# Both feed-forward products of a retention block computed with one level of Strassen's algorithm

## The chip, the core and the metric

The kernel runs on one core of a Trainium2 chip. The metric is device time in microseconds (us), from the launch of the program to its end on that core. The core has a matrix engine (PE, with the weight loads shown as PEld), a vector engine (DVE), a scalar engine (ACT), a general engine (POOL), and a queue (SP) that issues the transfers between DRAM and on-chip memory. PE reads its operands from on-chip memory and writes to eight banks of accumulators (PSUM), each 512 float32 wide on 128 partitions; DVE and ACT read these banks.

## What is computed

```python
# q, k, v: (4, 8, 768, 64); w_in: (512, 2048); w_out: (2048, 512)
for t in range(S):
    state = gamma * state + einsum('bhd,bhe->bhde', k[:, :, t], v[:, :, t])
    y[:, :, t] = scale * einsum('bhd,bhde->bhe', q[:, :, t], state)
x = y.transpose(0, 2, 1, 3).reshape(3072, 512)
h = x @ w_in
g = where(h > 0, h, exp(minimum(h, 0)) - 1)     # ELU
out = g @ w_out
```

Each head has its own decay gamma. All values are float32. The weights arrive as 64-bit floats and are turned into 32-bit floats on the chip, by integer operations on their two halves ("decoding").

## The kernel before

The 3072 tokens are cut into 24 chunks of 128 for the attention and into 6 blocks of 512 for the feed-forward part; a block is four chunks. For a chunk, `scores` (L189) multiplies keys and queries, DVE masks the result into `pt` (L192), and `values` multiplies `pt` with the values (L212), adds the contribution of the running state (L230), updates that state (L221 on PE, L243 to L246 on DVE) and writes one quarter of the block's input `xt` (L236). The scores have two PSUM banks of their own (`ps_s`), the values two others (`ps_y`), the state one (`ps_c`), the feed-forward products three (`ps_f`).

For a block, `ffn` computes 16 feed-forward tiles, each four matmuls of 128x128 weights with 512 tokens (L257), and turns each into `g` with one exponential on ACT (L262) and two operations on DVE (L263, L265). Then come 4 output tiles, each 16 matmuls with 512 columns of `w_out` (L273), a copy out of PSUM on ACT (L280) and a store. PE runs every float32 matmul as two passes, each with its own weight load, so a block has 128 passes of each product and the kernel 1536.

The order of the work is written out: Python generators issue the instructions, and each engine works through its own in that order. `ffn` yields after every feed-forward tile and every quarter of an output tile, 32 times a block; the loop at the end puts one chunk of the next block's attention into every eighth of these steps, and issues that chunk's loads on SP.

The weights come as 32 pieces of 128 x 512 words. `decode` needs one operation on ACT (L107), four on DVE (L110 to L114) and an integer addition on POOL (L115) for each. The first four pieces are decoded between the first four chunks, before any feed-forward tile; the others two at a time, after each of the first block's feed-forward tiles. `scale_v` multiplies a chunk's values by the inverse decay, on DVE for the first four chunks and on POOL (L176) after that.

Of the kernel before, what the change touches and what calls it, by code (L numbers as in the profile page):

```python
# [8 lines left out]
FP32 = mybir.dt.float32  # L9
# [7 lines left out]
def kernel(  # L17
# [3 lines left out]
    w_bits: bass.AP,  # L21
    out: bass.AP,
    dims,
):

# [14 lines left out]
    TB = 512  # L40
    HP = H // 2
# [4 lines left out]
    KJ = DM // P  # L46
    NFT = DFF // P
    assert D == 64 and DM == H * D == 512 and KJ == HP == 4 and S % C == 0 and NTOK % TB == 0
# [5 lines left out]
    ldpool = ctx.enter_context(tc.tile_pool(name="ldpool", bufs=4))  # L54
    wraw = ctx.enter_context(tc.tile_pool(name="wraw", bufs=4))
    wtmp = ctx.enter_context(tc.tile_pool(name="wtmp", bufs=2))
    ppool = ctx.enter_context(tc.tile_pool(name="ppool", bufs=2))
    spool = ctx.enter_context(tc.tile_pool(name="spool", bufs=2))
    xpool = ctx.enter_context(tc.tile_pool(name="xpool", bufs=2))
    gpool = ctx.enter_context(tc.tile_pool(name="gpool", bufs=NFT + 2))  # L60
    epool = ctx.enter_context(tc.tile_pool(name="epool", bufs=2))
    opool = ctx.enter_context(tc.tile_pool(name="opool", bufs=2))
    ps_s = ctx.enter_context(tc.tile_pool(name="ps_s", bufs=2, space=PSUM))
    ps_y = ctx.enter_context(tc.tile_pool(name="ps_y", bufs=2, space=PSUM))
    ps_c = ctx.enter_context(tc.tile_pool(name="ps_c", bufs=1, space=PSUM))
    ps_f = ctx.enter_context(tc.tile_pool(name="ps_f", bufs=3, space=PSUM))
# [5 lines left out]
    def load(m):  # L72

        if m >= NCHUNK:
            return
        qk = ldpool.tile([P, 2, HP, C], FP32, name="qk", tag="qk")
        nc.sync.dma_start(qk.rearrange("p a h c -> p (a h c)"), qkv[m, :, 0:1024])
        kv = ldpool.tile([C, 2, H, D], FP32, name="kvn", tag="kvn")
# [4 lines left out]

    w_in_sb = [const.tile([P, KJ, P], FP32, name=f"w_in{f}") for f in range(NFT)]
    w_out_sb = [const.tile([P, DM], FP32, name=f"w_out{f}") for f in range(NFT)]
    pieces = [w.rearrange("p a b -> p (a b)") for w in w_in_sb] + list(w_out_sb)
    NPIECE = len(pieces)
    staged, decoded = [], []

    def load_piece():  # L90
        n = len(staged)
        if n < NPIECE:

            t = wraw.tile([P, 512, 2], U32, name="wraw", tag="wraw")
            nc.sync.dma_start(t.rearrange("p c w -> p (c w)"), w_bits[n].bitcast(U32))
            staged.append(t)

    def decode(upto):
# [3 lines left out]
        vec = nc.vector  # L102
        while len(decoded) < min(upto, NPIECE):
            t, dst = staged[len(decoded)], pieces[len(decoded)].bitcast(U32)
            lo, hi = t[:, :, 0], t[:, :, 1]
            r = wtmp.tile([P, 512], U32, name="wr", tag="wr")
# [241 lines left out]
```

## Times and profile before

| | |
|---|---|
| time, median of 3 runs | 791.96 us (789.93 to 792.26) |
| time of the profiled execution | 793.54 us |
| its span, first to last instruction | 791.6 us |
| PE busy | 754.7 us, 95% |
| DVE, ACT, POOL busy | 251.5, 94.3 and 64.7 us |
| mean granted clock of PE | 0.987 |

Times in the rows are microseconds from the start of the span unless marked ns. A busy PE is not PE at its peak: the duration of a matmul in the trace (592 ns for 512 columns) holds its way through the array, during which the next one already runs. The pace of the passes is read from where successive ones start, or from a chain of waits, whose pieces don't overlap. PEld shows the weight loads beside the passes. An engine's idle time counts only where another engine waits for it.

### The profile page before, as it was taken

The page shows a single profiled execution, that of the slowest core. Times are in us where ns is not written, and L with a number is a line of the kernel's source. Part 1 is how long each engine was busy: PE and PEld are TensorE (multiplying, and loading weights), DVE is VectorE, ACT ScalarE, POOL GpSimd, SP SyncE. Part 2 cuts the span into 40 slices and gives each one's busy share as a digit, 9 for nine tenths or more (in the row PEclk, how much of TensorE's full clock was granted, in tenths as well). Part 3 has the DMA queues.
Part 4 walks back from the last instruction along what each step waited for, and adds up shares of the span by engine and source line. Part 5 has one row for each costly group of instructions (what it writes and reads, how often), then busy time and mean ns, then how long its engine had stood idle before and what let it go on. Part 6 is the DMA issues. An engine that isn't in the chain of part 4 may idle for free.

```text
span 791.6 us, 7134 instructions
## 1 busy us (share of the span) xinstructions
PE 754.7 (95%) x2944; PEld 358.9 (45%) x2944; DVE 251.5 (32%) x484; ACT 94.3 (12%) x158; POOL 64.7 (8%) x60
## 2 busy tenths in 40 slices
PE   6876669999999999999999999999999999999998
PEld 6432224444444444444544444444444444444443
DVE  6999994012342001333100433100333101133000
ACT  2222221001110000111000111000111000111000
POOL 1433443000000000000000000000000000000000
PEclk9999898999999999999999999999999999999999
DMA  9846450210101101101102001111000000000000
GB/s 344 325 157 211 159 187 0 80 64 17 54 8 46 67 26 67 53 1 54 66 14 80 28 26 53 45 37 67 14 1 0 3 24 14 13 1 0 14 13 26
DMA packets 15007, 48.68 MB, mean 61 GB/s; under 512 B 1664, under 2 KB 1664, under 8 KB 14976
## 3 DMA queue, kind: packets, MB, share of 16 engines
q1 hardware_dynamic: 14976, 48.24, 17.3%
q8 instruction: 23, 0.38, 0.2%
q14 instruction: 8, 0.07, 0.0%
HBM read 41.94 MB, written 6.29 MB: 61 GB/s over the span
## 4 chain that ended last, share of the span: by engine, by line
PE 86%; DVE 10%; issue 2%; DMA 2%; SPq 0%; ACT 0%; ACTq 0%
PE op L273 43%; PE hp L257 35%; DVE wc L112 3%; PE sc L189 3%; PE y L212 3%; DVE wc L110 2%; DVE wc L113 2%; DVE wc L114 1%; PE y L230 1%; PE kv L221 1%; DMA kvn<-in_qkv_dram 1%; DMA qk<-in_qkv_dram 1%; DVE pt L192 1%; DVE e L263 1%; DVE xt L236 0%
## 5 line engine op out<-in xcount | busy, mean ns | idle before, releaser
L257 PE MATMUL hp<-xt,w_in 128*128 128x512 f32 x768 | 342.3, 602 | 21.7 <-DVE g L265 21.1
L273 PE MATMUL op<-w_out,g 128*128 128x512 f32 x768 | 339.0, 599 | 3.0 <-DVE g L265 3.0
L257 PEld LDWEIGHTS hp<-xt,w_in 128*128 128x128 f32 x768 | 145.2, 192 | 204.0 <-issue 201.8
L273 PEld LDWEIGHTS op<-w_out,g 128*128 128x128 f32 x768 | 145.2, 191 | 182.1 <-issue 180.5
L263 DVE TENSOR_SCALAR e<-e 128x512 f32<-128x512 f32 x96 | 42.2, 439 | 242.6 <-ACT e L262 242.6
L262 ACT ACTIVATE e<-hp 128x512 f32<-128x512 f32 x96 | 57.1, 596 | 263.3 <-PE hp L257 263.3
L265 DVE TENSOR_TENSOR g<-hp,e 128x512 f32<-128x512 f32 x96 | 66.4, 692 | 4.0
L192 DVE TENSOR_TENSOR pt<-sc,cmask 128x512 f32<-128x512 f32 x48 | 30.8, 684 | 115.4 <-PE sc L189 115.4
L280 ACT COPY ot<-op 128x512 f32<-128x512 f32 x24 | 14.1, 586 | 351.3 <-PE op L273 351.3
L176 POOL TENSOR_TENSOR kvn<-kvn,vf 128x512 f32<-128x512 f32 x20 | 21.3, 1071 | 406.6 <-DMA kvn<-in_qkv_dram 378.8
L236 DVE TENSOR_TENSOR xt<-y,etab 128x256 f32<-128x256 f32 x48 | 18.4, 419 | 112.0 <-PE y L230 91.7
L189 PE MATMUL sc<-qk 64*128 64x128 f32 x384 | 30.6, 298 | 6.3 <-DMA qk<-in_qkv_dram 5.7
L189 PEld LDWEIGHTS sc<-qk 64*128 64x128 f32 x384 | 25.6, 198 | 22.3 <-issue 15.2
L107 ACT ACTIVATE wr<-wraw 128x512 uint32<-128x512 uint32 x32 | 21.8, 681 | 78.5 <-POOL w_out L115 33.6
L212 PE MATMUL y<-pt,kvn 128*64 128x128 f32 x384 | 27.8, 290 | 2.3 <-DVE xt L236 2.3
L212 PEld LDWEIGHTS y<-pt,kvn 128*64 128x64 f32 x384 | 21.7, 142 | 18.2 <-issue 13.9
L112 DVE TENSOR_SCALAR wc<-wc 128x512 f32<-128x512 f32 x32 | 27.6, 863 | 1.1
L115 POOL TENSOR_TENSOR w_in<-wc,wr 128x512 uint32<-128x512 uint32 x16 | 21.5, 1344 | 48.0 <-DVE wc L114 44.2
L115 POOL TENSOR_TENSOR w_out<-wc,wr 128x512 uint32<-128x512 uint32 x16 | 21.0, 1312 | 30.6 <-DVE wc L114 28.6
L114 DVE SCALAR_TENSOR_TENSOR wc<-wraw,wc 128x512 uint32<-128x512 uint32 x32 | 22.2, 693 | 1.1
L110 DVE TENSOR_SCALAR wc<-wraw 128x512 uint32<-128x512 uint32 x32 | 17.0, 531 | 0.1
L113 DVE TENSOR_SCALAR wc<-wc 128x512 uint32<-128x512 uint32 x32 | 13.7, 427 | 1.1
(26 smaller groups left out, 73.9 us busy)
## 6 DMA issues: line engine op xcount, KB each, us to landing
wraw<-in_w_dram SPq DMA_DIRECT2D x32, 512.0 KB, 3.3
qk<-in_qkv_dram SPq DMA_DIRECT2D x24, 512.0 KB, 4.1
kvn<-in_qkv_dram SPq DMA_DIRECT2D x24, 512.0 KB, 4.9
out_dram<-ot SPq DMA_DIRECT2D x24, 256.0 KB, 2.0
```

The lines of the kernel that those rows point to most:

```text
L110: vec.tensor_scalar(c, hi, 0x7FFFFFFF, None, ALU.bitwise_and)
L112: vec.tensor_scalar(cf, cf, 122879.9921875, 2.0**-15, ALU.min, ALU.max)
L114: vec.scalar_tensor_tensor(c, hi, 0xC0000000, c, ALU.bitwise_and, ALU.bitwise_or)
L115: nc.gpsimd.tensor_tensor(out=dst, in0=c, in1=r, op=ALU.add)
L189: nc.tensor.matmul(sc[a][:, p, :], lhsT=qk[r, 1, p, :], rhs=qk[r, 0, p, :], start=True, stop=True)
L192: nc.vector.tensor_tensor(out=pt[:, a], in0=sc[a], in1=cmask.unsqueeze(1).to_broadcast([C, HP, C]), op=ALU.mult)
L212: nc.tensor.matmul(y[a][c * D : (c + 1) * D, u, :], lhsT=vn[:, h, :], rhs=pt[:, a, p, :], start=(u == 0), stop=(i == 0), skip_group_check= ...
L257: nc.tensor.matmul(hp, lhsT=w_in_sb[ft][:, j, :], rhs=xt[:, j, :], start=(j == 0), stop=(j == KJ - 1))
L262: nc.scalar.activation(e, hp, AF.Exp)
L263: nc.vector.tensor_scalar(e, e, 1.0, -1.0, ALU.min, ALU.add)
L265: nc.vector.tensor_tensor(out=gt, in0=hp, in1=e, op=ALU.max)
L273: nc.tensor.matmul(op, lhsT=g[ft][:, c * P : (c + 1) * P], rhs=w_out_sb[ft], start=(ft == 0), stop=(ft == NFT - 1),)
```

## The change

The first block keeps the ordinary products. From the second block on, both products are cut in halves on all three sides, and seven products of the halves replace eight: the left and right sides are the quarters of the weights and of the input, or sums and differences of quarters, and the results are combined afterwards. The seven are called 1 to 7; `strassen` issues them in the order 1, 2, 6, 7, 5, 3, 4.

- For `h = x @ w_in` (`first`), the 16 tiles are taken four at a time, as n = 0 to 3. A product is four matmuls of 128x128 weights with 256 tokens, 8 passes. Three accumulators (pa, pb, pd) hold two tiles of 128 x 256 each. ACT copies three intermediate sums out of pa (m1, u2, u4), DVE adds them to the results of 2, 5 and 4 (`plus`, L347), and ELU takes two operations on ACT (L280, L281) and one on DVE (L283) for each of the results C11, C22, C12 and C21. Two more operations on DVE make the differences T3 and T1 (L403). Products 3 and 4 of one n are issued after products 1 and 2 of the next one.
- For `out = g @ w_out` (`second`), each product is 16 matmuls, 32 passes. Its weights, 1 MB, are fetched from a DRAM scratch (`fetch`, L418) into three buffers that the raw weights used before. The four chunks of attention for the next block stand behind products 2, 6, 7 and 5.
- The first block's second product (`plain_second`) takes the pieces of `w_out` as they are decoded, keeps four accumulators open, forms the combinations of `w_out` on DVE (L313, four operations of 128x256 for each of eight pieces) and writes both to the scratch; `combine_w_in` forms those of `w_in` in place (L329, four operations of 128x512 for each n). All four chunks of the second block's attention stand in this product.
- A piece of weights is now 128 x 1024 words, 16 in all. `decode` uses two operations on ACT and four on DVE, the last being the integer addition (L130), and none on POOL. Two pieces are decoded between the first four chunks, eight during the first product, six during the second. ELU's new form also holds in the first block.
- The decay is no longer applied chunk by chunk to the state: the tables `vf` and `etab` hold it for all 768 positions, the state accumulates in PSUM, and ACT copies it out. Scores and values share two PSUM banks after the first block (tag "s"), and the feed-forward products have five.

```diff
+    def decode():
+        n = len(decoded)
...
+        nc.scalar.activation(cf, hi.bitcast(FP32), AF.Abs)
+        vec.tensor_scalar(cf, cf, 122879.9921875, 2.0**-15, ALU.min, ALU.max)
+        vec.tensor_scalar(c, c, 3, 0x3FFFFFF8, ALU.logical_shift_left, ALU.bitwise_and)
+        vec.scalar_tensor_tensor(c, hi, 0xC0000000, c, ALU.bitwise_and, ALU.bitwise_or)
+        nc.scalar.activation(flat, lo, AF.Copy, scale=2.0**-29)
+        vec.tensor_tensor(out=flat, in0=c, in1=flat, op=ALU.add)
...
+        ps, tag = (ps, "f") if ps else (ps_s, "s")
+        y = [ps.tile([P, 2, C], FP32, name="y", tag=tag) for _ in range(2)]
...
+    def elu(g, h):
+        r = epool.tile([P, 512], FP32, name="r", tag="r")
+        nc.scalar.activation(r, h, AF.Relu, scale=-1.0)
+        nc.scalar.activation(r, r, AF.Exp, scale=-1.0)
+        flush()
+        later.append(lambda: nc.vector.scalar_tensor_tensor(g, r, -1.0, h, ALU.add, ALU.max))
...
+    def strassen(product, use, between):
+        yield
+        pa = bank()
+        product(1, pa, True)
+        m1 = kept(pa)
+        yield
+        pb = bank()
+        product(2, pb, True)
+        use("C11", plus(pb, m1))
+        yield
+        product(6, pa, False)
+        u2 = kept(pa)
+        yield
+        pd = bank()
+        product(7, pd, True)
+        yield
+        product(5, pa, False)
+        u4 = kept(pa)
+        use("C22", plus(pd, u4))
+        yield "gap"
+        product(3, pa, False)
+        use("C12", pa)
+        yield
+        product(4, pd, False)
+        use("C21", plus(pd, u2))
...
+            elu(flat(g), flat(h))
+            gq[name] = g
+            if name == "C12":
+                flush()
+                t3_ = gpool.tile([P, 2, TH], FP32, name="g", tag="g")
+                sub(t3_, gq["C22"], gq["C12"])
+                sub(gq["C12"], gq["C12"], gq["C11"])
...
+    for tb in range(1, NTB):
+        gqs = [{} for _ in range(NQ)]
+        for n in range(NQ):
+            cur = first(n, gqs[n])
+            for at in range(3):
+                next(cur)
+            for _ in tail:
+                pass
+            for s in cur:
+                if s == "gap":
+                    break
+            tail = cur
+        cur = second(tb, gqs)
+        next(cur)
+        next(cur)
+        for _ in tail:
+            pass
+        flush()
+        m = (tb + 1) * CPB
+        scale_v(m)
+        scores(m)
+        for j in range(4):
+            s = next(cur)
+            scale_v(m + j + 1) if j < 3 else None
+            values(m + j)
+            load(m + j + 2)
+            if j < 3:
+                scores(m + j + 1)
```

In the orders below one row is a float32 matmul, not one of its two passes. On PE, before, a feed-forward tile is one row of four matmuls with 512 columns:

```order
L257 MATMUL hp<-xt,w_in_99 128x512 x4
L257 MATMUL hp<-xt,w_in_100 128x512 x4
L189 MATMUL sc<-qk 128x128 x8
L257 MATMUL hp<-xt,w_in_101 128x512 x4
```

Now, for n = 1 of a block's first product; ps_997 is pa and ps_1021 is pd of n = 0, ps_1039, ps_1046 and ps_1087 are pa, pb and pd of n = 1:

```order
L390 MATMUL ps_1039<-xb_168,w_a1_94 128x256 x4
L390 MATMUL ps_1046<-xb_168,w_a1_94 128x256 x4
L390 MATMUL ps_997<-xb_168,w_s0_101 128x256 x4
L390 MATMUL ps_1021<-xt3_172,w_b0_97 128x256 x4
L390 MATMUL ps_1039<-xt1_170,w_s1_102 128x256 x4
L390 MATMUL ps_1087<-xt2_171,w_s1_102 128x256 x4
L390 MATMUL ps_1039<-xt0_169,w_b1_98 128x256 x4
```

The matmuls now have half as many columns, and stand as products 1, 2 of n = 1, 3, 4 of n = 0, and 6, 7, 5 of n = 1.

On ACT, in the same place: the copies m1 (m_1044), u2 (m_1085) and u4 (m_1096) of n = 1, and between them the ELU steps of C11 of n = 1 (r_1054), C12 (r_1063, from PSUM) and C21 (r_1078) of n = 0:

```order
L342 COPY m_1044<-ps_1039 128x512
L280 ACTIVATE r_1054<-h_1051 128x512
L281 ACTIVATE r_1054<-r_1054 128x512
L280 ACTIVATE r_1063<-ps_997 128x512
L281 ACTIVATE r_1063<-r_1063 128x512
L280 ACTIVATE r_1078<-h_1075 128x512
L281 ACTIVATE r_1078<-r_1078 128x512
L342 COPY m_1085<-ps_1039 128x512
L342 COPY m_1096<-ps_1039 128x512
```

Before, ACT had one operation for a feed-forward tile; here the copy u2, for which product 5 waits, stands behind six ELU steps.

On PE, in a block's second product, around the second chunk of attention (one row of L427 is a product):

```order
L427 MATMUL ps<-g,ws 128x256 x16
L227 MATMUL y<-pt,kvn 64x128 x8
L237 MATMUL kv<-kvn 64x64 x8
L247 MATMUL y<-qk,state 64x128 x8
L204 MATMUL sc<-qk 128x128 x8
L427 MATMUL ps<-g,ws 128x256 x16
```

Before, matmuls of the feed-forward part stood between one chunk's values and the next chunk's scores; now the scores (L204) follow the values directly, in the same two banks.

## Rows read from the trace of the kernel before

**Rows 1.** Page, part 1: busy time, share of the span, instructions; part 4: chain.

```profile
PE 754.7 (95%) x2944; PEld 358.9 (45%) x2944; DVE 251.5 (32%) x484; ACT 94.3 (12%) x158; POOL 64.7 (8%) x60
...
PE 86%; DVE 10%; issue 2%; DMA 2%; SPq 0%; ACT 0%; ACTq 0%
```

**Rows 2.** Chain of waits in order of time: start us, us, what.

```profile
119.44 10.13 PE op L273 x16
...
184.18 6.87 PE hp L257 x16
...
678.22 54.93 PE hp L257 x128
733.15 54.95 PE op L273 x128
```

**Rows 3.** Timeline of PE, first 120 us: start, us, instructions [idle before <-releaser].

```profile
27.08 7.11 PE L257 MATMUL hp<-xt,w_in 128*128 128x512 f32 x16 [0.61 <-DVE xt L236]
...
52.90 3.67 PE L257 MATMUL hp<-xt,w_in 128*128 128x512 f32 x8 [1.41 <-DVE g L265]
59.23 3.67 PE L257 MATMUL hp<-xt,w_in 128*128 128x512 f32 x8 [2.65 <-DVE g L265]
...
112.80 3.67 PE L257 MATMUL hp<-xt,w_in 128*128 128x512 f32 x8 [2.66 <-DVE g L265]
```

**Rows 4.** Timeline of DVE: one feed-forward step's two pieces, and two small operations.

```profile
2.61 0.23 DVE L161 CAST post<-pos_t 128x128 f32<-128x128 int32 x1
...
46.34 0.77 DVE L110 TENSOR_SCALAR wc<-wraw 128x512 uint32<-128x512 uint32 x1
...
47.61 0.43 DVE L113 TENSOR_SCALAR wc<-wc 128x512 uint32<-128x512 uint32 x1
...
52.67 0.77 DVE L110 TENSOR_SCALAR wc<-wraw 128x512 uint32<-128x512 uint32 x1
```

**Rows 5.** Timeline at 141 us: 16 passes of 128 columns.

```profile
141.09 0.85 PEld L212 LDWEIGHTS y<-pt,kvn 128*64 128x64 f32 x16 [0.76 <-issue]
141.09 1.09 PE L212 MATMUL y<-pt,kvn 128*64 128x128 f32 x16
...
142.01 0.64 PE L221 MATMUL kv<-kvn 128*64 128x64 f32 x16
```

**Rows 6.** Timeline at 750 us: passes of 512 columns and their weight loads.

```profile
749.73 6.60 PE L273 MATMUL op<-w_out,g 128*128 128x512 f32 x15
750.16 0.19 PEld L273 LDWEIGHTS op<-w_out,g 128*128 128x128 f32 x1 [0.24 <-issue]
750.59 0.19 PEld L273 LDWEIGHTS op<-w_out,g 128*128 128x128 f32 x1 [0.24 <-issue]
```

**Rows 7.** Page, part 5: costliest groups, busy us, mean ns of one, idle before.

```profile
L262 ACT ACTIVATE e<-hp 128x512 f32<-128x512 f32 x96 | 57.1, 596 | 263.3 <-PE hp L257 263.3
L265 DVE TENSOR_TENSOR g<-hp,e 128x512 f32<-128x512 f32 x96 | 66.4, 692 | 4.0
L192 DVE TENSOR_TENSOR pt<-sc,cmask 128x512 f32<-128x512 f32 x48 | 30.8, 684 | 115.4 <-PE sc L189 115.4
L280 ACT COPY ot<-op 128x512 f32<-128x512 f32 x24 | 14.1, 586 | 351.3 <-PE op L273 351.3
...
L236 DVE TENSOR_TENSOR xt<-y,etab 128x256 f32<-128x256 f32 x48 | 18.4, 419 | 112.0 <-PE y L230 91.7
...
L107 ACT ACTIVATE wr<-wraw 128x512 uint32<-128x512 uint32 x32 | 21.8, 681 | 78.5 <-POOL w_out L115 33.6
...
L115 POOL TENSOR_TENSOR w_in<-wc,wr 128x512 uint32<-128x512 uint32 x16 | 21.5, 1344 | 48.0 <-DVE wc L114 44.2
...
L114 DVE SCALAR_TENSOR_TENSOR wc<-wraw,wc 128x512 uint32<-128x512 uint32 x32 | 22.2, 693 | 1.1
```

**Rows 8.** Timelines at 733 and 173 us: handing over between engines.

```profile
732.99 3.60 PE L273 MATMUL op<-w_out,g 128*128 128x512 f32 x8
733.19 0.60 ACT L262 ACTIVATE e<-hp 128x512 f32<-128x512 f32 x1 [2.84 <-PE hp L257]
733.82 0.43 DVE L263 TENSOR_SCALAR e<-e 128x512 f32<-128x512 f32 x1 [2.21 <-ACT e L262]
...
173.72 0.76 DVE L236 TENSOR_TENSOR xt<-y,etab 128x256 f32<-128x256 f32 x2 [11.30 <-PE y L230]
```

**Rows 9.** Page, part 6: DMA issues, KB each, median us to landing.

```profile
wraw<-in_w_dram SPq DMA_DIRECT2D x32, 512.0 KB, 3.3
...
out_dram<-ot SPq DMA_DIRECT2D x24, 256.0 KB, 2.0
```

More of the change, by code (lines that the diff above doesn't have):

```diff
@@ L21 @@
     w_bits: bass.AP,
+    scratch: bass.AP,
     out: bass.AP,
@@ L184, in scores @@
         qk, kv = raw[m]
-        sc = [ps_s.tile([C, HP, C], FP32, name="sc", tag="sc") for _ in range(2)]
+        sc = [ps_s.tile([C, HP, C], FP32, name="sc", tag="s") for _ in range(2)]
         for p in range(HP):
@@ new lines, in values, with combine_x, flush @@
+            nc.scalar.activation(held["state"], held["kv"], AF.Copy, scale=scale)
+    half = [slice(0, TH), slice(TH, TB)]
+    def combine_x():
+        sub = lambda o, x, y: nc.vector.tensor_tensor(out=o, in0=x, in1=y, op=ALU.subtract)
+        b11, b12, b21, b22 = (xb[:, 2 * r : 2 * r + 2, half[t]] for r in range(2) for t in range(2))
+        sub(xt[0], b12, b11)
+        sub(xt[1], b22, xt[0])
+        sub(xt[2], b22, b12)
+        sub(xt[3], b21, xt[1])
+    later = []
+    def flush():
+        while later:
+            later.pop(0)()
@@ new lines, in combine_w_in, with bank, kept @@
+    def combine_w_in(n):
+        tt = lambda o, x, y, op: nc.vector.tensor_tensor(out=o, in0=x, in1=y, op=op)
+        a11, a12, a21, a22 = w_a[n][:, 0], w_a[n][:, 1], w_b[n][:, 0], w_b[n][:, 1]
+        s2, s3, s4 = (w_s[n][:, j] for j in range(3))
+        tt(s3, a11, a21, ALU.subtract)
+        tt(a21, a21, a22, ALU.add)
+        tt(s2, a21, a11, ALU.subtract)
+        tt(s4, a12, s2, ALU.subtract)
+    def bank():
+        return ps_f.tile([P, 2, TH], FP32, name="ps", tag="f")
+    def kept(ps):
+        m = mpool.tile([P, 2, TH], FP32, name="m", tag="m")
+        nc.scalar.copy(m, ps)
+        return m
@@ new lines, in first, with product @@
+    def first(n, gq):
+        a11, a12, s1, a22 = w_a[n][:, 0], w_a[n][:, 1], w_b[n][:, 0], w_b[n][:, 1]
+        s2, s3, s4 = (w_s[n][:, j] for j in range(3))
+        b11, b12, b21, b22 = (xb[:, 2 * r : 2 * r + 2, half[t]] for r in range(2) for t in range(2))
+        t1, t2, t3, t4_ = xt
+        pairs = {1: (a11, b11), 2: (a12, b21), 3: (s4, b22), 4: (a22, t4_), 5: (s1, t1), 6: (s2, t2), 7: (s3, t3)}
+        def product(j, ps, begin):
+            w, x = pairs[j]
+            for fi in range(2):
+                for j2 in range(2):
@@ new lines @@
+    combine_x()
+    for j in ORDER2[:3]:
+        fetch(1, j)
+    tail = iter(())
+    for tb in range(1, NTB):
+        gqs = [{} for _ in range(NQ)]
+        for n in range(NQ):
+            cur = first(n, gqs[n])
[12 more added lines that the diff above has]
+            pass
+        flush()
+        m = (tb + 1) * CPB
+        scale_v(m)
+        scores(m)
+        for j in range(4):
+            s = next(cur)
[4 more added lines that the diff above has]
+                scores(m + j + 1)
+        assert s == "gap"
+        for _ in cur:
+            pass
+        combine_x() if tb + 1 < NTB else None
+        tail = iter(())
```

315 lines of the change are left out of this document (183 added, 132 removed).

## The prediction, made before the changed kernel was run

> **What bounds the kernel now.** I read the page's busy times first: PE is busy 95% of the span, DVE 32%, ACT 12%, and the chain that ended last runs 86% on PE and 10% on DVE [rows 1]. Then the chain in order of time, to see where the two parts lie [rows 2]. The reader is to see three stretches. Up to 119.4 us the first block's first product goes on; from 119.4 to 184.2 its second one, with the next block's attention in between; from there on every block takes the same time, (678.22 − 184.18) / 4 = 123.5 us with four chunks of attention, and the last, without attention, 54.93 + 54.95 = 109.9. So a chunk costs PE (123.5 − 109.9) / 4 = 3.4 us. The timeline of PE shows the first stretch from inside [rows 3]: the first feed-forward tile starts at 27.1 us, but a tile comes only every 6.33 us (52.90 to 59.23), 3.67 us of work and 2.65 us of waiting for DVE. DVE is full there with two pieces of decoding per tile: its pattern repeats every 6.33 us too, 46.34 to 52.67 [rows 4]. So up to 119.4 us DVE's decoding sets the time, and after that the passes of PE, one every 54.93 / 128 = 0.429 us.
>
> **The passes.** From the second block on, 5 blocks lose 256 passes of 512 columns each, 1280 × 0.429 = 549.3 us, and get 2 × 7 × 32 = 448 passes of 256 columns, 2240 in all. No pass in the trace has 256 columns. From below, half of 0.429 is 0.2146. From the other side, 16 passes of 128 columns, which run two at a time on halves of the columns, take 142.01 − 141.09 = 0.92 us, 0.115 per pair [rows 5]; the straight line through 128 and 512 columns gives 0.22 for 256. I take 0.216, nearer to the long passes, since the first pair of the 16 is slow: 2240 × 0.216 = 483.8, a gain of 65.5 us (57 to 69).
>
> That holds only if a weight load stays hidden behind a pass half as long. A load takes 0.19 us, begins with the pass before it and leaves 0.24 us free, while passes follow at 0.43 [rows 6]; 0.19 fits into 0.216 with 0.026 to spare. In the short passes each pair has two loads of 64 columns, and 16 of these end in 0.85 us beside 1.09 us of passes [rows 5]. A rule speaks against the change: the Trainium skill ("TensorE: Matmul & The Clock Gate", Part 3, Packing small matmuls) says that loads overlap running matmuls only when they aim at another row group. Here both use all 128 rows; by that rule the trace's loads would stand in the open, and rows 5 and 6 show them covered. I take the rows, and keep the other case as a rival.
>
> **The first block.** A piece of 1024 words now costs DVE four operations. At 512 columns the two short kinds take 0.43 [rows 4], at 128 such an operation takes 0.23, so 0.69 at 1024 by the straight line; the long kind takes 0.693, and 0.419 at 256 [rows 7], so 1.24 at 1024. The integer addition has not run on DVE. Its bounds are 1.24, as another two-operand operation of DVE, and 2 × 1.34 = 2.69, as POOL needs for two pieces of 512 [rows 7]; I take 1.24, the row of the same engine. A piece: 2 × 0.69 + 2 × 1.24 = 3.9 us (5.3 at the upper bound). In the first product DVE has one piece and two ELU operations of 0.69 per two tiles, 5.3 us (6.7), and PE 16 passes, 6.87: PE is late there, no longer DVE. ACT has two operations per piece and four ELU steps at about 0.6, some 5 us. So 128 passes run back to back from about 27.1 us, where I leave the start: DVE decodes one long piece before the last chunk instead of three short ones, but 0.5 MB more is loaded ahead of that chunk. The first 16 passes of before took 7.11 instead of 6.87 [rows 3], so the product ends at 27.1 + 0.2 + 54.9 = 82.2 instead of 119.4.
>
> The second product has 54.95 us of passes and four chunks, 13.7. DVE per chunk: two pieces 7.8 (six pieces in all), combinations 8 × 0.42 for `w_out` and 4 × 0.69 for `w_in`, the chunk's own two operations of `pt` 1.3 [rows 7] and two of `xb` 0.8: 16.0 us against 13.7 + 3.4 = 17.1 of PE. That just fits, and with the upper bound for the addition it is 18.9, 1.8 us over for each of three chunks. Where DVE's work hides, it hides behind these passes. At the end the next block waits for its last quarter of input, 0.2 us to hand over and 0.76 for `xb` [rows 8], 1.0. The block ends at 82.2 + 54.95 + 13.7 + 1.0 = 151.9 instead of 184.2: a gain of 32.3 us, at the upper bound 27.
>
> **The new waits.** (a) In a block's first product a product of the seven takes PE 8 × 0.216 = 1.73 us, and product 5 may start only when ACT has copied u2. I follow one n from the end of product 5 of the n before. Product 2 ends at 3.46 and is seen 0.2 us later, as ACT sees a tile 0.2 after the next stream starts [rows 8]. Then, each behind the other by the order on ACT and DVE: C11's `plus` 0.69, its two steps on ACT 1.2, C12's two steps 1.2, C12's g 0.69, T3 and T1 1.38, C21's `plus` 0.69, its two steps 1.2, the copy u2 0.59 [rows 7]: 7.6 us and eleven hand-overs of 0.03, the gap between the end of ACT's step and DVE's start [rows 8]: done at 11.65. Product 5 comes up after six products, at 10.38. PE waits 1.25 us. Behind product 5 stand the next n's products 1 and 2. It happens for n = 1, 2 and 3 (n = 0 has no products 3 and 4 before it): 15 × 1.25 = 18.8 us. If steps on ACT that read on-chip memory take 0.68, as L107 does, it is 1.75 each, 26 in all; if ACT overlaps them more, 0.8 and 12. (b) In the second product the next chunk's scores need the banks that the values leave: hand-over and two `xb`, 0.2 + 0.76, of which some 0.1 is the usual change of operands: 0.9 us, for three chunks of four blocks, 10.8 us (0 to 13). (c) In the last block, without attention, product 3 waits for the copy u4: 0.2 + 0.59 + 0.03, 0.8 us. The weights from the scratch: 1 MB as 16 × 128 x 8 runs of 1 KB. Four times 256 KB in 2.0 us [rows 9] is 8 us; a piece is asked for two products, 13.8 us and mostly two chunks, before it is needed. It stays hidden.
>
> **The sum.** −65.5 − 32.3 + 18.8 + 10.8 + 0.8 = −67.4 us. Against the profiled execution's own 793.5 that gives 726.1; this execution lies 1.6 us above the median of the runs, 791.96. I forecast 726.
>
> **The rivals.**
> 1. The waits don't come about: ACT and DVE run ahead, and the copies and the banks are ready. For it: both are idle for more than half of such a stretch. Against: the order on ACT is fixed and u2 is behind six steps. Then 726 − 30 = 697.
> 2. Decoding still bounds the first block: for example the addition needs the whole 2.69, or the raw weights come late. For it: it does so now. Against: per word DVE has less to do. Half of the gain would go: 742; all of it: 758.
> 3. Slower: the weight loads are not hidden. Every pass of 256 columns then takes up to 0.19 more, 2240 × 0.19 = 426 us, 1152 in all. The change turns into a loss from 67 / 2240 = 0.03 us per pass. That is the rule named above. Against it: rows 5 and 6, in which they are hidden. A load that only just fits and costs 0.01 gives 748.
> 4. The fetch is late: with runs of 1 KB a piece would have to need over 20 us, more than twice the row's rate; at 25 us the second product takes four such pieces, 100 us instead of 65, and five of them cost 175: 900. Nothing in the rows speaks for it but the shorter runs.
>
> **How the numbers follow.** The forecast with its sized waits has 0.68; its own terms reach from −57 − 27 + 26 + 13 + 1 = −44 (749) to −69 − 33 + 12 + 0 + 1 = −89 (704). Rival 1 has 0.12, rival 2 0.10, rival 3 0.06 (0.05 of it above 0.03 us per pass), rival 4 0.03; 0.01 is for no change, which would need the gain and the waits to cancel. A measurement of this kernel can tell about 0.3% from no change. Faster: 0.68 + 0.12 + 0.10 + 0.01 = 0.91; slower 0.08; same 0.01. The range is 700 to 758: it leaves out rival 1's best case and what is slower.
>
> **What would show it.** Right: the first feed-forward passes near 27 us and the first product's end near 82 us with no idle time of DVE's making; the first block's end near 152; passes of 256 columns 0.216 us apart, with loads of 0.19 beside them; in each block three waits of about 1.2 us before product 5, ended by ACT's copy (L342); about 1 us before `scores` (L204), ended by `xb`; a block of about 117 us, the last 101. Wrong: passes of 0.23 us or more; PE waiting for DVE's decoding after 30 us; PE waiting for the fetches (L418); a block without the waits of (a).

## The result and the profile after

The changed kernel takes 729.64 us (median of 4 runs, 727.12 to 730.78), the kernel before 792.11 beside it: a ratio of 0.9206, 95% interval 0.9168 to 0.9245. The forecast was 726 in a range from 700 to 758. The profiled execution took 728.61, its span 726.8.

The page of the changed kernel, busy times and then the chain by engine, against [rows 1]:

```profile
PE 687.1 (95%) x3904; PEld 542.2 (75%) x3904; DVE 317.0 (44%) x504; ACT 208.3 (29%) x332; POOL 23.4 (3%) x28
...
PE 68%; DVE 14%; ACT 12%; issue 4%; DMA 2%; SPq 0%; DVEq 0%; ACTq 0%
```

PE's share is the same 95%, of a shorter span, so the share alone hides what happened. The chain shows it: 12% now runs over ACT, which had 0%. The chain in order of time, against [rows 2], with the starts of blocks 3 and 6 and the last product:

```profile
274.70 8.65 PE ps L390 x40
...
621.61 8.65 PE ps L390 x40
...
680.62 27.64 PE ps L427 x128
708.92 14.10 PE ps L427 x64
```

L390 is the first product (`x @ w_in`), L427 the second (`g @ w_out`). 40 passes in 8.65 us are 0.216 each, and 128 in 27.64 are 0.2159. Blocks 3 to 5 take (621.61 − 274.70) / 3 = 115.6 us each, against 123.5 before, and the last one 723.0 − 621.6 = 101.4, against 109.9.

The timeline of PE in the first block, against [rows 3]; the bracket is the idle time before the row and what ended it:

```profile
27.73 7.13 PE L292 MATMUL hp<-xb,w_a 128*128 128x512 f32 x16 [0.52 <-DVE xb L252]
...
82.76 2.74 PE L308 MATMUL op<-g,wo 128*128 128x512 f32 x6
87.92 6.25 PE L308 MATMUL op<-g,wo 128*128 128x512 f32 x10 [2.42 <-DVE g L283]
...
155.20 3.72 PE L390 MATMUL ps<-xb,w_a 128*128 128x256 f32 x16
```

The 2.65 us of waiting for DVE at every tile are gone: 128 passes stand from 27.73 to 82.76. At 82.76 the second product starts, and stops after six passes until DVE has made a g (L283), which was not forecast. By the code it is not the value of g that is missing: six passes begin three accumulators, and the fourth takes the PSUM bank of the last tile but one, which that L283 still has to read. The chain leads there through DVE's steps for a piece of weights, the last of which (L130) starts at 86.04. The ten passes behind the stop take 6.25 us, where ten at 0.429 take 4.3. The windows there show why (after the busy times come granted clock, DMA share, GB/s):

```profile
86.00:90.00 4.00, 2.08 (x3) 0.96 (x4) 3.93 (x8) 1.58 (x2) 0.00 (x0) 0.81 0.73 184
90.00:94.10 4.10, 4.10 (x8) 1.43 (x6) 3.68 (x4) 0.00 (x0) 0.00 (x0) 0.77 1.14 364
```

PE stood still for 2.42 us, and after that the granted clock is 0.81 and 0.77: part of these stretches is at the lower level, 1.2 GHz. The wait costs 2.4 us of idle time and 1.9 of slow passes, 4.3 in all. Block 2 begins at 155.20 instead of 184.18.

The timeline of PE for one n of a block's first product (n = 1 of block 3):

```profile
294.68 1.99 PE L390 MATMUL ps<-xt,w_b 128*128 128x256 f32 x8 [0.98 <-ACT m L342]
...
308.01 1.99 PE L390 MATMUL ps<-xt,w_b 128*128 128x256 f32 x8 [0.99 <-ACT m L342]
```

The rows with a bracket are product 5, which waits for the copy u2 (L342). From one to the next, 308.01 − 294.68 = 13.33 us pass. Seven products back to back would take 7 × 8 × 0.2159 = 12.09. The loss is 1.24 us; 0.98 of it shows as idle time, 0.10 is a slower start after it, and the rest is the end of the pass before, which another pass would have overlapped. The chain of waits leading to one of them, in time (start, us, what; the rows left out are short hand-overs, most of them named "issue", and two stretches of 0.5 and 0.6 us, named so too, in which the second step of C11's ELU and the second difference run):

```profile
286.88 0.70 DVE h L347
...
287.61 0.64 ACT r L280
...
288.81 0.59 ACT r L280
289.42 0.64 ACT r L281
...
290.08 0.70 DVE g L283
290.80 0.70 DVE g L403
...
292.14 0.69 DVE h L347
...
292.86 0.64 ACT r L280
293.52 0.63 ACT r L281
294.15 0.48 ACT m L342
```

It is the very series that was forecast: `plus` of C11 (L347), four ELU steps on ACT (three of them shown), the g of C12 (L283), the differences (L403), `plus` of C21, its two steps on ACT, and only then the copy u2: 7.75 us from 286.88 to the copy's end at 294.63.

The group of the page that answers to [rows 6], and the fetch, which answers to [rows 9] (KB each, median us to landing):

```profile
L427 PEld LDWEIGHTS ps<-g,ws 128*128 128x128 f32 x1120 | 211.1, 190 | 31.6 <-ACT m L342 1.1
...
ws<-scratch_dram SPq DMA_DIRECT2D x35, 1024.0 KB, 5.7
```

A weight load still takes 190 ns and its passes stand 216 ns apart. 1 MB in runs of 1 KB lands in 5.7 us, below the 8 that were estimated.

PE's waits by cause (total us, times, longest):

```profile
PE ps L390 <- ACT m L342: 17.3, 16, 2.5
...
PE sc L204 <- DVE xb L252: 5.1, 10, 0.5
...
PE ps L427 <- ACT m L342: 0.7, 1, 0.7
```

The copies in the first product cost 17.3 us of idle time: 15 times about 0.98 for u2, and 2.5 of another wait in block 2. The scores wait ten times for the banks, and the last row is the copy u4 in the last block.

That other wait, in the timeline of all engines at block 2's n = 0:

```profile
162.40 0.69 DVE L347 TENSOR_TENSOR h<-ps,m 128x512 f32<-128x512 f32 x1 [2.62 <-DMA out_dram<-ot]
...
164.94 1.35 PE L390 MATMUL ps<-xt,w_b 128*128 128x256 f32 x5 [2.52 <-ACT m L342]
```

DVE's first `plus` of the block needs a buffer of `hpool`, and the first block's output tiles `ot` share that pool (tag "h"): it waits 2.62 us for the store of one, and PE 2.52 behind it.

The integer addition, which had not been on DVE before, in the timeline of DVE:

```profile
78.98 1.23 DVE L130 CUSTOM_DVE_ANT_0 wo<-wc,wo 128x2048 uint16<-128x2048 uint16 x1
```

It takes 1.23 us for 128x1024 words (shown as twice as many of half the size).

### The profile page after: what moved, and what is told of

Its sections match the earlier page's. It is cut to its first block, busy times and chain, and to the rows that moved or that the text cites. A ratio compares the mean times of both kernels' runs of the same rounds, so it can differ in the third digit from the quotient of the medians.

```text
span 726.8 us, 9254 instructions
## 1 busy us (share of the span) xinstructions
PE 687.1 (95%) x3904; PEld 542.2 (75%) x3904; DVE 317.0 (44%) x504; ACT 208.3 (29%) x332; POOL 23.4 (3%) x28
## 4 chain that ended last, share of the span: by engine, by line
PE 68%; DVE 14%; ACT 12%; issue 4%; DMA 2%; SPq 0%; DVEq 0%; ACTq 0%
PE ps L427 34%; PE ps L390 16%; PE op L308 8%; ACT r L280 5%; PE sc L204 4%; DVE h L347 3%; PE y L227 3%; ACT r L281 3%; DVE g L403 2%; DVE g L283 2%; ACT m L342 2%; PE y L247 2%; DVE wc L128 2%; DMA qk<-in_qkv_dram 1%; ACT wc L124 1%
## 5 line engine op out<-in xcount | busy, mean ns | idle before, releaser
L427 PE MATMUL ps<-g,ws 128*128 128x256 f32 x1120 | 248.3, 381 | 0.7 <-ACT m L342 0.7
L427 PEld LDWEIGHTS ps<-g,ws 128*128 128x128 f32 x1120 | 211.1, 190 | 31.6 <-ACT m L342 1.1
L347 DVE TENSOR_TENSOR h<-ps,m 128x512 f32<-128x512 f32 x75 | 51.7, 689 | 228.0 <-ACT m L342 140.4
L342 ACT COPY m<-ps 128x512 f32<-128x512 f32 x75 | 43.3, 577 | 193.5 <-PE ps L427 116.3
L390 PE MATMUL ps<-xt,w_b 128*128 128x256 f32 x320 | 77.3, 384 | 17.3 <-ACT m L342 17.3
L390 PEld LDWEIGHTS ps<-xt,w_b 128*128 128x128 f32 x320 | 59.5, 190 | 31.1 <-ACT m L342 23.7
L390 PE MATMUL ps<-xb,w_a 128*128 128x256 f32 x320 | 72.4, 379 | 0.0
L390 PE MATMUL ps<-xt,w_s 128*128 128x256 f32 x320 | 72.4, 379 | 0.0
L390 PEld LDWEIGHTS ps<-xt,w_s 128*128 128x128 f32 x320 | 60.7, 190 | 8.4 <-issue 0.2
L390 PEld LDWEIGHTS ps<-xb,w_a 128*128 128x128 f32 x320 | 60.7, 190 | 8.4 <-issue 0.2
L280 ACT ACTIVATE r<-h 128x512 f32<-128x512 f32 x60 | 37.8, 630 | 101.3 <-DVE h L347 101.3
L281 ACT ACTIVATE r<-r 128x512 f32<-128x512 f32 x96 | 60.5, 630 | 3.0
L308 PE MATMUL op<-g,wo 128*128 128x512 f32 x128 | 58.9, 613 | 2.4 <-DVE g L283 2.4
L283 DVE SCALAR_TENSOR_TENSOR g<-r,h 128x512 f32<-128x512 f32 x60 | 41.1, 686 | 22.0 <-ACT r L281 22.0
L204 PE MATMUL sc<-qk 64*128 64x128 f32 x384 | 33.5, 300 | 11.9 <-DMA qk<-in_qkv_dram 6.8
L204 PEld LDWEIGHTS sc<-qk 64*128 64x128 f32 x384 | 28.4, 198 | 19.8 <-DVE xb L252 7.6
L207 DVE TENSOR_TENSOR pt<-sc,cmask 128x512 f32<-128x512 f32 x48 | 30.9, 685 | 21.5 <-PE sc L204 21.3
L390 PE MATMUL ps<-xb,w_s 128*128 128x256 f32 x160 | 37.8, 379 | 0.0
```

The costliest lines, as they stand in the source:

```text
L204: nc.tensor.matmul(sc[a][:, p, :], lhsT=qk[r, 1, p, :], rhs=qk[r, 0, p, :], start=True, stop=True)
L207: nc.vector.tensor_tensor(out=pt[:, a], in0=sc[a], in1=cmask.unsqueeze(1).to_broadcast([C, HP, C]), op=ALU.mult)
L280: nc.scalar.activation(r, h, AF.Relu, scale=-1.0)
L281: nc.scalar.activation(r, r, AF.Exp, scale=-1.0)
L283: later.append(lambda: nc.vector.scalar_tensor_tensor(g, r, -1.0, h, ALU.add, ALU.max))
L308: nc.tensor.matmul(ops[d], lhsT=wo[:, row, d * P : (d + 1) * P], rhs=gs[row * NF + f], start=(f == 0 and row == 0), stop=(f == NF - 1 and ...
```

## Experiments

The theory: the time is the sum of PE's passes, the first block's faster decoding, and a few waits of PE, each of about 1 us, on places that can be named: u2 in the first product (15), the scores' banks in the second one (10), and once each the start of the first block's second product, the store in block 2, and u4 in the last block. The rivals are those of the prediction. Every kernel was timed against the kernel before on the same chip, and the ratios are to that; where a difference from the changed kernel is given, it is taken from 729.64. The runs behind this number span 3.7 us, and the kernel before's medians differ by up to 1.6 us between the chips, so such a difference is good to about 2 us, and what is finer is read from the traces.

**Whole parts: the blocks without Strassen.** The changed kernel with ordinary products in every block; `w_out` decoded into 8 tiles of its own, and no combinations, scratch or fetches. What the edit takes out and changes, in part:

```diff
-            dst = t4.tile([P, 2, 512], FP32, name="wo", tag="t4")
+            dst = w_o[n - 2 * NQ]
...
-    def strassen(product, use, between):
...
-    def second(tb, gqs):
```

> Edit: the changed kernel without Strassen: all six blocks use ordinary products with 512 columns, the weights of w_out stay on chip, no combinations are formed and nothing goes through the scratch; decoding, ELU, tables, state and the banks are those of the changed kernel; each chunk of attention is spread over the second product. Theory: the gain has two parts, some 30 us from the first block, which is no longer bound by decoding, and some 36 us net from Strassen. This kernel keeps the first alone: first block to about 152 to 155 us, four blocks of 123.5, one of 109.9, 3.5 at the end, a span of about 762, some 30 us below the kernel before (ratio 0.962) and 35 above the changed one. Rival: Strassen's passes alone make the gain, and the first block is faster because of them: then this kernel stands within 8 us of the kernel before.

765.27 us (763.97 to 766.69), ratio 0.9657 (0.9627 to 0.9687). Its chain in time:

```profile
157.19 54.93 PE hp L290 x128
```

The first block ends at 157.2, as in the changed kernel within 2 us, and the passes are those of [rows 2] again. So 184.2 − 157.2 = 27 us of the gain come from the first block, with the attention's new form, and 765.27 − 729.64 = 35.6 from the products of halves, their waits paid.

**The load behind a shorter pass.** The kernel before, with each matmul of 512 columns split into two of 256, so that twice as many loads do the same work (the first product's matmuls are shown; the second's are cut in the same way):

```diff
-                nc.tensor.matmul(
-                    hp, lhsT=w_in_sb[ft][:, j, :], rhs=xt[:, j, :], start=(j == 0), stop=(j == KJ - 1)
-                )
+                for c in range(2):
+                    cols = slice(c * 256, (c + 1) * 256)
+                    nc.tensor.matmul(
+                        hp[:, cols], lhsT=w_in_sb[ft][:, j, :], rhs=xt[:, j, cols],
+                        start=(j == 0 and c == 0), stop=(j == KJ - 1), skip_group_check=True,
+                    )
```

> Edit: the kernel before, with each matmul of both products cut into two of 256 columns, each with its own weight load; the arithmetic is the same, with twice as many passes, 3072 of 256 columns for 1536 of 512. Theory: a load of 0.19 us hides behind a pass of 0.216; the passes take 3072 x 0.216 = 663.6 us where they took 659.1, and the time rises by 4 us or less (some of the extra passes lie in the first product, which waits for decoding): ratio to the kernel before 1.00 to 1.006. Rival: loads stand in the open by 0.03 us or more: at least 90 us slower; wholly, 3072 x 0.19 = 580 us slower.

794.41 us (793.16 to 797.46), ratio 1.0034 (1.0016 to 1.0052). The last block in its chain:

```profile
736.78 55.27 PE op L278 x256
```

55.27 / 256 = 0.2159 us per pass, against 0.2146 for half of a long one. Loads of full arrays, all on the same rows, stay hidden; rival 3 is out. The rule of the Trainium skill that stood behind it ("TensorE: Matmul & The Clock Gate", Part 3, Packing small matmuls), that a load overlaps a running matmul only on another row group, would have put up to 0.19 us on each of these passes; the trace disagrees with it (the section also lets a load aimed at a background weight buffer go ahead, and no run here shows where a load goes).

**How much room was left.** The same with four matmuls of 128 columns, timed once:

```diff
-                for c in range(2):
-                    cols = slice(c * 256, (c + 1) * 256)
+                for c in range(4):
+                    cols = slice(c * 128, (c + 1) * 128)
```

> Edit: the kernel before with each matmul cut into four of 128 columns, each with its own load of 128 columns on all rows: 6144 passes. One look, to find how long a load must be alone. Theory: the 0.19 us of a load in the records hold a way in that overlaps the next load, as 16 loads on halves of the rows come 0.11 apart; a pass of 128 columns then takes 0.11, and the last block without attention 256 x 4 x 0.11 = 113 us instead of 109.9. Rival: loads follow one another at 0.19: 1024 x 0.19 = 195 us for that block, and 256 columns were near the limit.

817.6 us. Its chain, and the loads in its timeline:

```profile
754.93 57.19 PE op L278 x512
```

```profile
759.91 1.75 PEld L278 LDWEIGHTS op<-w_out,g 128*128 128x128 f32 x15
```

57.19 / 512 = 0.1117 us per pass, 0.107 being a quarter of a long one. Passes with full loads can follow at 0.112, so the 0.19 us that a load takes in the trace is no room it needs: 15 loads stand in 1.75 us where 15 × 0.19 would be 2.85, so the records of successive loads overlap. What a load does in the 0.19 us is not shown. A pass of 256 columns had at least 0.10 us to spare, not the 0.026 of the prediction.

**Wait (a): the copy ahead of the ELU steps.** C21's ELU steps, and with them its g, are held back until after the copy u2 is issued:

```diff
         u2 = kept(pa)
+        run_held()
...
-            elu(flat(g), flat(h))
-            gq[name] = g
...
+            def finish():
+                g = gpool.tile([P, 2, TH], FP32, name="g", tag="g")
+                elu(flat(g), flat(h))
+                gq[name] = g
...
+            if name == "C21":
+                held_back.append(finish)
+            else:
+                finish()
```

The same call stands behind the tail of products 3 and 4 in the second product.

> Edit: in the first product the ELU of C21 (two steps on ACT, one on DVE) is issued after the copy u2 of the next n, not before it; nothing else moves. Theory: product 5 waits for u2 because u2 stands on ACT behind C21's two steps, which wait for DVE's C12, T3, T1 and plus; the changed kernel shows 13.33 us per n where its passes take 7 x 1.727 = 12.09, 1.24 us for three n of five blocks. Then the wait goes, n takes 12.1 us and the span falls by about 15 x 1.24 = 18.6 us, to about 708 (ratio to the changed kernel 0.974). Rival: another wait is as late as this one (product 7 for C12's accumulator, or product 5 for ACT's backlog of C21 moved behind): then n stays above 13 us and less than 5 us is gained. Second rival: the change of order delays C21 for the second product, and the loss moves there.

712.56 us (711.6 to 713.31), ratio 0.8991 (0.8966 to 0.9016), 17.1 below the changed kernel. Its timeline of PE:

```profile
26.53 9.25 PE L292 MATMUL hp<-xb,w_a 128*128 128x512 f32 x16 [0.51 <-DVE xb L252]
...
165.96 2.46 PE L397 MATMUL ps<-xt,w_b 128*128 128x256 f32 x8 [2.70 <-ACT m L348]
168.21 4.88 PE L397 MATMUL ps<-xb,w_a 128*128 128x256 f32 x16
...
282.12 3.62 PE L397 MATMUL ps<-xb,w_a 128*128 128x256 f32 x16
...
294.21 3.62 PE L397 MATMUL ps<-xb,w_a 128*128 128x256 f32 x16
```

From one n to the next, 294.21 − 282.12 = 12.09 us pass instead of 13.33, and no row between has a bracket: all 15 waits are gone and nothing takes their place, so the cause was the place of C21's ELU steps ahead of the copy. The sum of the waits is 15 × 1.24 = 18.6; the medians give 17.1, the profiled spans 726.8 − 710.8 = 16.0. The rest in the profiled execution is the clock, by the windows of this kernel:

```profile
26.00:31.00 5.00, 4.49 (x9) 1.95 (x7) 4.50 (x6) 1.50 (x2) 0.00 (x0) 0.52 0.11 15
...
165.00:170.00 5.00, 4.04 (x13) 3.35 (x14) 0.93 (x2) 1.69 (x4) 0.00 (x0) 0.73 1.09 361
```

The first 16 passes run almost wholly at the lower level (0.52) and take 9.25 us, 2.1 more than in the changed kernel; behind the wait of 2.70 us in block 2, 24 passes take 1.7 more (2.46 and 4.88 against 1.99 and 3.62) at 0.73. The first pass comes 1.2 us earlier: 18.6 + 1.2 − 2.1 − 1.7 = 16.0. Both slow stretches are in this execution and not in the profiled one of the changed kernel; the edit has no part in the first. Where the chip lowers the clock is not the same from run to run: in the changed kernel the wait of 2.52 us in block 2 went by at 1.00.

**Wait (b): the scores later.** A chunk's `scores` are issued in the midst of the next product instead of ahead of it:

```diff
             for f in range(NF):
+                if f == 2:
+                    while mid:
+                        mid.pop(0)()
...
-                scores(m + j + 1)
+                mid.append(lambda k=m + j + 1: scores(k))
```

> Edit: in the second product of blocks 2 to 5 the next chunk's scores are issued after the first quarter of the following product, not directly after the values. Theory: the scores wait for the two banks that the values leave, 0.6 us before the first one and 0.4 us for the second, in the changed kernel for 10 of 12 places; with 1.7 us of passes in between the banks are free, and the span falls by about 10 us, to about 717 (ratio to the changed kernel 0.986). Rival: the wait is an ordinary change of operands of PE, and stays wherever the scores stand: no change within 2 us.

722.46 us (721.35 to 723.61), ratio 0.9117 (0.9089 to 0.9144), 7.2 less. The timeline of PE after a chunk's values, the changed kernel first:

```profile
354.31 1.48 PE L204 MATMUL sc<-qk 64*128 64x128 f32 x16 [0.51 <-DVE xb L252]
...
365.50 1.49 PE L204 MATMUL sc<-qk 64*128 64x128 f32 x16 [0.51 <-DVE xb L252]
```

and then this kernel:

```profile
353.56 2.00 PE L431 MATMUL ps<-g,ws 128*128 128x256 f32 x8
355.49 1.16 PE L204 MATMUL sc<-qk 64*128 64x128 f32 x16
...
365.97 1.16 PE L204 MATMUL sc<-qk 64*128 64x128 f32 x16
```

Eight passes now stand where PE waited for the banks that the values leave, and the scores behind them find theirs free. The changed kernel's trace has ten such waits, 0.51 us of idle time each and a slower start behind it (1.48 us for the 16 passes, 1.16 here). From one chunk's scores to the next 365.50 − 354.31 = 11.19 us pass there and 365.97 − 355.49 = 10.48 here: 0.71 a place, 7.1 for ten, and the medians give 7.2. Of the twelve places that were forecast, two show no wait.

**All waits at once.** Both edits, and the two that came only once: `ot` in another pool, and a third buffer for ELU's r:

```diff
-    epool = ctx.enter_context(tc.tile_pool(name="epool", bufs=2))
+    epool = ctx.enter_context(tc.tile_pool(name="epool", bufs=3))
...
-            ot = hpool.tile([P, 2, TH], FP32, name="ot", tag="h")
+            ot = t4.tile([P, 2, TH], FP32, name="ot", tag="t4")
```

> Edits: C21's ELU behind u2 and the scores a quarter of a product later, both as in the two experiments before; besides, the first block's output tiles get buffers of the pool that holds the decoded weights (in the changed kernel the second block's first n waits 2.5 us for the store of one), and the ELU has three buffers r instead of two (in the first product DVE and ACT take 7.05 us per two tiles in a ring where PE takes 6.87, which ends in a wait of 2.4 us). Theory: the four waits are independent and add up: 15 x 1.24 + 10 x 0.75 + 2.5 + 2.4 = 31 us, a time of about 699 (ratio to the changed kernel 0.958). Rival: some of them hide one another, PE waits elsewhere, and the time stays above 705.

698.06 us (697.95 to 698.23), ratio 0.8818 (0.8797 to 0.8839), 31.6 less. At the second product's start, in the timeline of PE, 1.05 us of the 2.42 are left, and the ten passes behind it take 4.56:

```profile
87.43 4.56 PE L308 MATMUL op<-g,wo 128*128 128x512 f32 x10 [1.05 <-DVE g L283]
```

So this wait costs 3.1 us less (1.4 of idle time, 1.7 of clock), and the sum is 18.6 + 7.1 + 3.1 + 2.5 = 31.3, where the medians give 31.6. The profiled spans give 726.8 − 696.2 = 30.6: the first feed-forward pass comes 0.9 us earlier, at 26.82, and the first 16 take 8.92 us instead of 7.13, so 31.3 + 0.9 − 1.8 = 30.4 was to be expected there. To about 1 us, then, the waits add up, and none hides another. The cause of the one at 87.92 is seen on ACT in the changed kernel's first product:

```profile
66.77 0.60 ACT L280 ACTIVATE r<-hp 128x512 f32<-128x512 f32 x1 [2.58 <-DVE g L283]
...
73.83 0.60 ACT L280 ACTIVATE r<-hp 128x512 f32<-128x512 f32 x1 [2.57 <-DVE g L283]
```

and in this kernel's:

```profile
66.68 0.60 ACT L280 ACTIVATE r<-hp 128x512 f32<-128x512 f32 x1 [2.17 <-PE hp L292]
...
73.55 0.60 ACT L280 ACTIVATE r<-hp 128x512 f32<-128x512 f32 x1 [2.17 <-PE hp L292]
```

In the changed kernel ACT's Relu waits 2.6 us for one of two buffers r, which DVE's L283 frees, and the next piece's first step (L124, at 67.94) stands behind it. That ring repeats every 73.83 − 66.77 = 7.06 us, PE's two tiles every 6.87: the lag grows by 0.2 us per pair of tiles until PE meets it at the second product. With a third r, ACT waits for PE instead, and the period is 73.55 − 66.68 = 6.87. The 1.05 us that are left are seen on DVE: ACT has finished the ELU steps of the last tile but one at 81.67, but its L283 stands behind a whole piece of decoding, from L126 at 82.72 to L130 at 85.56, and starts at 86.70.

**The fetch's slack.** Every piece of `w_out`'s combinations is fetched twice into the same buffer:

```diff
         nc.sync.dma_start(t, scratch[:, :, 256 * SLOT[j] : 256 * SLOT[j] + 256].rearrange("f p d -> p f d"))
+        nc.sync.dma_start(t, scratch[:, :, 256 * SLOT[j] : 256 * SLOT[j] + 256].rearrange("f p d -> p f d"))
```

> Edit: the changed kernel, with each piece of w_out's combinations fetched twice, the second fetch into the same buffer after the first has landed (35 MB more, and the queue stands still for the first one). Theory: a piece lands 5.7 us after its issue and is asked for two products, 13.8 us or more, before PE needs it; twice that is still in time: less than 2 us of change. Rival: the stream is just in time, and each of 20 pieces that are fetched during the second product comes late by 3 us or more: 60 us slower.

735.74 us (732.97 to 738.42), ratio 0.9293 (0.9258 to 0.9329): 6.1 us more, where less than 2 was expected. Its waits (total, count, longest):

```profile
SPq L419 <- DMA ws<-scratch_dram: 235.1, 35, 10.1
...
PE sc L204 <- DMA qk<-in_qkv_dram: 11.7, 7, 4.8
...
PE ps L428 <- DMA ws<-scratch_dram: 2.6, 2, 1.7
```

The fetches themselves are late only twice, 2.6 us in all. But the second fetch may not overwrite the first before it has landed, so SP's queue stood still 35 times, 235.1 us, and the chunks' loads issued behind it came later: in block 3 one load of `qk` follows its fetch at 359.41, where the changed kernel has it at 353.88, while its time from issue to landing hardly changes (median 6.7 us against 6.5). So PE waits for `qk` at four places behind the first block, 5.9 us in all (the other 5.8 of the 11.7 lie before the first feed-forward pass, where the changed kernel waits 6.8). What the step missed is that an extra transfer also holds up its queue. Rival 4 is out all the same: with twice the traffic PE waits 2.6 us for it. At the four places the 0.5 us for the banks fall away, block 2 starts 1.0 us earlier, and its wait for the store is 0.5 longer: 2.6 + 5.9 − 2.0 − 1.0 + 0.5 = 6.0, and the profiled spans give 732.7 − 726.8 = 5.9.

**Where the first block's gain comes from.** Only the integer addition, moved from DVE back to POOL, where the kernel before had it:

```diff
-        vec.tensor_tensor(out=flat, in0=c, in1=flat, op=ALU.add)
+        nc.gpsimd.tensor_tensor(out=flat, in0=c, in1=flat, op=ALU.add)
```

> Edit: the changed kernel with the integer addition of the decoding on POOL, as in the kernel before. Theory: the first block gained because only half of the weights are decoded in its first product, one piece of 1024 words per two tiles instead of four of 512, and not because the addition moved: DVE loses 1.23 us per piece, POOL takes about 2.7, hidden; PE still sets the pace, the time stays within 3 us of the changed kernel. Rival: the addition on POOL slows DVE's operations beside it (in the kernel before the operation of L112 took 1.38 us instead of 0.43 where POOL was adding), DVE's steps come to more than 6.87 us per two tiles again, and the first block is over 8 us longer.

723.75 us (722.43 to 724.64), ratio 0.9137 (0.9109 to 0.9165): 5.9 us less, where at most 3 of change were expected. The timeline of PE:

```profile
24.15 7.10 PE L292 MATMUL hp<-xb,w_a 128*128 128x512 f32 x16 [0.61 <-DVE xb L252]
...
79.16 7.03 PE L308 MATMUL op<-g,wo 128*128 128x512 f32 x16
```

The first pass comes 3.6 us earlier: the last chunk's values wait 1.67 us for DVE's masking (L207) instead of 3.04, as the addition no longer stands ahead of it; the passes behind that wait take 1.35 us less; and 0.9 is that all before it stands earlier. The wait at the second product's start is gone, with the 4.3 us that it cost; with two buffers r, ACT's steps now come every 6.87 us (62.19 to 69.06), so the ring was too slow only with the addition on DVE in it. 3.6 + 4.3 = 7.9 us are gained by the start of block 2; the store in block 2 then takes back a part:

```profile
158.49 3.78 PE L390 MATMUL ps<-xt,w_b 128*128 128x256 f32 x8 [4.06 <-ACT m L342]
```

That wait is 1.5 us longer, and the 24 passes behind it, at a granted clock of 0.65 to 0.67, take 2.3 more (3.78 and 4.22 against 1.99 and 3.62): 7.9 − 1.5 − 2.3 = 4.1, as the profiled spans give. So the addition's move to DVE is not what made the first block faster: it cost time. What remains for the gain, fewer operations per word on DVE and six of the pieces decoded beside the second product, no run takes apart. An estimate from the rows: 1024 words took DVE 5.2 us before (the two pieces from 46.34 to 52.67, without the ELU steps between them) and take 3.9 in the changed kernel. Half the words at the old price would give DVE 5.2 + 2.2 for ELU = 7.4 us per two tiles, and all of them at the new price 2 × 3.9 + 1.3 = 9.1. Both are above PE's 6.87, so by this estimate the changed kernel needed both.

**The best version.** All waits out and the addition on POOL, the edits shown above together.

> Edits: the four of the experiment that takes away all waits, and the integer addition on POOL, as in the experiment on it. Theory: the addition's 1.23 us on DVE stood once ahead of the last chunk's masking and so ahead of the first feed-forward pass (24.15 us with it on POOL, 27.73 in the changed kernel, 26.82 with all waits taken away), and the last 1.0 us of waiting at the second product's start goes with it: some 3.5 us less, about 694.5. Rival: POOL's additions slow DVE's combinations beside them (one took 1.72 us instead of 0.43), the second product of the first block waits for them, and nothing is gained.

692.45 us (692.25 to 692.83), ratio 0.8757 (0.873 to 0.8783), 37.2 below the changed kernel and 5.6 below the kernel without waits, where 3.5 were expected. The timeline of PE:

```profile
24.23 7.10 PE L292 MATMUL hp<-xb,w_a 128*128 128x512 f32 x16 [0.60 <-DVE xb L252]
```

All of it lies in the first block, which ends at 147.29 instead of 153.02. The first pass comes 2.6 us earlier (26.82 there) and the wait at the second product's start is gone, as expected; most of what comes beyond that is the first 16 passes, 7.10 us instead of 8.92, that is, the clock. That 31.6 + 5.9 = 37.5 is so near 37.2 is chance: both parts hold the wait at the second product's start, and the second lost 3.8 us at the store, which here doesn't wait. PE is busy 98% of the span (677.9 us), and behind the first block it waits for nothing but u4, 0.7 us.

## Why the prediction was right

It was right in mechanism and, within 4 us, in size. That it came so near is in part luck: the first block's gain was forecast 3.3 us too large and a wait of 2.5 us overlooked, while the scores' waits were priced 3.7 us too high. Step by step:

- **Passes**: forecast −65.5 us at 0.216 each; measured 0.2159, −65.7. That the load stays hidden was right; its reason, 0.19 just fitting into 0.216, was not: 0.112 is enough.
- **First block**: forecast 184.2 to 151.9, measured 155.2; the gain is 29.0, not 32.3. The product from 27.1 to 82.2 came from 27.73 to 82.76, with DVE's wait gone, as worked out. The integer addition, whose bounds were 1.24 and 2.69, takes 1.23. The step that failed is the second product's: it took 72.4 us and was forecast at 54.95 + 13.7 + 1.0 = 69.7. The chunks took some 13.1. The 1.0 of handing over to block 2 didn't come, as its products 1 and 2 need only the first half of the tokens. But 4.3 us went into the wait at 87.92 and the clock behind it. The prediction had compared sums of busy time in the first product, DVE's 5.3 and ACT's 5 us against PE's 6.87, and not followed the ring of two buffers r that ties the two together, 7.06. Nor does any term of its sum price passes at the lower clock behind a wait, though [rows 2] show it: the 16 passes at 119.44 take 10.13 us where 16 at 184.18 take 6.87.
- **(a) u2**: forecast 15 × 1.25 = 18.8; measured 15 × 1.24 = 18.6, through the forecast series, and its removal gave 17.1 by the medians, with the clock taking back a part.
- **(b) scores' banks**: forecast 12 × 0.9 = 10.8; measured 10 places, 7.1 in all. Each is 0.2 us less, and two of the twelve don't wait.
- **(c) u4**: forecast 0.8, measured 0.7.
- **Not foreseen**: 2.5 us in block 2, for the store of `ot`. The pool's shared tag stood in the code; the sum has no term for it.

From block 2 on, −65.7 + 18.6 + 7.1 + 0.7 + 2.5 = −36.8; the chains give a gain of (788.1 − 184.18) − (723.0 − 155.20) = 36.1. The forecast for the same stretch was −35.1.

Of the rivals, 1 (the waits don't come) is refuted by the 15 rows ended by the copy, and the kernel without them takes 698.06, near the 697 that it gave (726 − 30 is 696), though by way of a slower first block and of waits that it did not count; 2 by the first product, where PE no longer waits for decoding, but a little of it came true at 87.92, where PE waits for an L283 behind a piece of weights on DVE, 4.3 us; 3 by the passes at 0.2159 and 0.1117; 4 by the fetch at 5.7 us and by the doubled one. A fetched piece is 128 × 8 runs of 1 KB, not 16 times as many as the prediction writes; its 8 us don't depend on that.

## What to carry to other kernels

A Strassen level takes away an eighth of the passes' time (549.3 to 483.6 us here), but it makes a chain of small steps between the engines. So count the chain, not the busy shares: here ACT was idle for 71% of the span and still set PE's pace, because one copy stood behind six ELU steps in a fixed order. Issue first what another engine waits for, and give a ring of buffers one more where two engines' steps alternate. Of a pool that is shared by two kinds of tiles, ask which store must land before the next tile is written.

## What the runs showed of the hardware

- Float32 passes with a full 128x128 load follow each other at 0.429 us for 512 columns, 0.2159 for 256 and 0.1117 for 128, although a load shows as 0.19 us; at 128 columns the records of successive loads overlap. So a load's time in the records is no bound for the pass that hides it.
- A wait of PE can cost its length and as much again: after 2.42 us of standing still the granted clock was 0.77 to 0.81 and ten passes took 1.9 us more, after 4.06 us the clock was 0.65 to 0.67 and 24 passes took 2.3 more. In the kernel before, 2.97 us at 119.44 cost the 16 passes behind it some 3.1, and 2.65 and 2.66 us at 59.23 and 112.80 cost nothing. After 1.05 us the clock stayed at 1.00. After the same 3.0 us of waiting for DVE ahead of the last chunk's values, the first 16 feed-forward passes took 7.13 us in the changed kernel, and 8.92 and 9.25 in two others. After 2.52 us the clock stayed at 1.00 in one execution, and after 2.70 at the same place it was 0.73 in another; what decides between these is open.
- A transfer that waits for its buffer holds what is issued behind it on the same queue: 35 second fetches kept SP's queue waiting 235.1 us, and a load of `qk` was issued 5.5 us later for it.
- A fetch of 1 MB in runs of 1 KB lands in 5.7 us, less than four times the 2.0 us of a 256 KB store in the kernel before. Size alone does not set it: in the changed kernel a store of 256 KB takes 5.8.
